# One tuned attention and feed-forward block: how rounded q and k travel to DRAM, and which engine turns four layer norms

## The chip, the cores and the metric

The program runs on one core of one Trainium2 chip. The metric is the device time of one execution in microseconds (us). Three executions of the kernel before took 732.46, 733.01 and 734.0 us; their median is 733.01 us. A profile was taken of one further execution.

## The reference

One transformer block on 2048 tokens of 448 features, in float32:

```python
def _A_ref(x, wqkv, wo):
    B, S, D = x.shape
    H = 16; Dh = D // H; W = 256
    qkv = ((x @ wqkv).reshape(B, S, 3, H, Dh)).transpose(2, 0, 3, 1, 4)
    q, k, v = qkv[0], qkv[1], qkv[2]
    scores = jnp.einsum("bhqd,bhkd->bhqk", q, k) * (Dh ** -0.5)
    mask = (i - j >= 0) & (i - j < W)
    p = _softmax(jnp.where(mask, scores, -1e9))
    o = jnp.einsum("bhqk,bhkd->bhqd", p, v)
    return o.transpose(0, 2, 1, 3).reshape(B, S, D) @ wo

h  = x + _A_ref(_layernorm(x), A_wqkv, A_wo)
n  = _layernorm(h)
h2 = h + (gelu(n @ w_gate) * (n @ w_up)) @ w_down      # 448 -> 1792 -> 448
```

There are 16 heads of 28 features, and a query sees the 256 tokens that end with itself.

## The kernel before

**Precision.** Matmuls run on a rounded float32 type (`F32R`). To keep float32 accuracy each operand is split in a high part (a copy rounded by ScalarE, `to_hi`, L342) and a low part (the rest, `to_lo`, L345, on VectorE or GpSimd), and a product is the sum of high x high, high x low and low x high. For q and k the three partial products sit side by side in the contraction: q is stored as (high, low, high) and k as (high, high, low), so that one matmul of 84 rows (3 x 28) makes a score tile.

**Stages.** The tokens go in 4 chunks (c) of 512, the heads in 4 groups (g) of 4. A block B = 4c + g is one chunk and one group, B = 0 to 15. Per chunk:

- `layer_norms` and `normalise` (L360, L387) make the normalised tokens of a 128-token tile t in `xn`, and its transpose in `xT`, high and low part. There are two ways. A tile that is not in `TURNED` is transposed by TensorE: four matmuls against `ident` (L398) into a PSUM bank, from which ScalarE takes the high part (L423) and VectorE the low part (L408, L409). A tile in `TURNED` goes through `turn` (L429): VectorE transposes 32x32 blocks into the other `xn` buffer (L435), four DMAs write them to DRAM in the right places (L439), two DMAs read the transposed tile back into `xT` (L441, L443), and then ScalarE makes the high part in three instructions (L447 to L449) and VectorE the low part in two (L452, L453). The layer norms ahead of the feed-forward (`kind == "ln2"`) always go through `turn`.
- `project_tile(c, m)` (L598) makes one of the 7 q and k tiles of a chunk: 11 matmuls (L609) into a PSUM bank, the high part by ScalarE (L613), the low part by VectorE (L614), both into a staging buffer that `pk_at` (L584) hands out in turn, and then DMAs to DRAM (`put`, L617). Even m are q of a group, odd m are k; each tile also holds 16 rows of k of the last group. There are two staging buffers in `proj`; tiles 2 and 3 (`PKX`) use a place in `pp`.
- `loads(B)` (L629) reads q and k of the block back from DRAM into `rq` and `rk` (L639), 84 rows by 4 heads.
- `scores` (L649) computes scores for the row maxima alone (matmul L657, VectorE L661), `maxima` (L671) turns these and puts them beside q (matmul L688), `probs` (L721) computes the scores again, transposed and with the maximum taken off (matmul L729), and ScalarE takes exp into `pp` (L733); `select` (L738) masks on GpSimd; `attend` (L753) multiplies by v (L763); `drain` and `output` divide and project (L788 to L810).

**Feed-forward.** 14 weight records of 128 columns; `product` (L954) does gate and up (L969 for the first four, L945 after them), gelu, and the down product, with VectorE adding to `hres` (L1047). Records 0 and 1 are fetched into `raw` (L864), record 2 through a DRAM copy (L857, key `FETCH`); their split is in `weight_splits` (L866). The first four products may run while attention is still going; they read records 0 and 1.

**What sets the order.** Every piece of work is an `op` with an engine, an estimated cost, a priority key and its dependences. `Lists.run` (L129) plays all of them through a model of the core while the program is built: again and again it takes, of all engines, the operation that can start first, the smallest key among those that can start at nearly the same moment, and emits it. So the instruction order of every engine, SyncE's DMA issues included, is fixed at build time by estimates; on the chip, semaphores only make an instruction wait. A block is 16 units of key. Constants shift keys:

```python
WIN = 14
LEAD = 90
LN1 = (0, -20, 70, 134)
LN2 = (166, 231)
FETCH = 200
PKX = (2, 3)
TURNED = (8, 9, 10, 11, 12, 13, 14, 15)
```

`WIN` is how far ahead of a block's need the matmuls of its projection begin (L608); `LN1[c]` is the key of the layer norms of chunk c; `LN2` and `LEAD` those of the layer norms ahead of the feed-forward.

**PSUM.** Eight banks of 128 x 512. `allowed` (L1132) says which kind of work may take which: until projections are done, scores have banks 0 and 1, probabilities 2 and 3, the attention sums 4 and 5, and layer norms that TensorE turns, v, projections and the output share 6 and 7.

Of the kernel before, what the change touches and what calls it, by code (L numbers as in the profile page):

```python
# [9 lines left out]
F32R = mybir.dt.float32r  # L10
# [18 lines left out]
WT = 7  # L29
# [6 lines left out]
LAG_P = 15  # L36
LAG_V = 10
EDGE = 8
WIN = 14
FFN = 1000  # L40
LEAD = 90
MARGIN = 0.8
START = 0.8
EARLY = 2
# [1 line left out]
HOLDO = 1  # L46
AHEAD = 7
BEHIND = 5
LN1 = (0, -20, 70, 134)
LN2 = (166, 231)  # L50
VKEY = (-30, -22, 14, 24)
VHALF = 0
FETCH = 200
POOLED = (3,)
PKX = (2, 3)
PAIRED = 4
TURNED = (8, 9, 10, 11, 12, 13, 14, 15)
SPANS = {"pp", "proj", "raw", "xT", "h", "rqf", "rkf", "vm", "rec0", "rec1", "rec2", "gh"}
SLOW = 9.0
WARM = 26.0  # L60
# [7 lines left out]
def mm(n):  # L68
    return max(n / 2400 + 0.0155, 0.115)
# [14 lines left out]
class Lists:  # L84
# [6 lines left out]
    def op(self, eng, cost, lat, key, fn, r=(), w=(), bank=None, port=False, size=0, tag=None, after=(), part=None):  # L91
        o = Op()
        o.eng, o.cost, o.lat, o.key, o.fn, o.port, o.size, o.tag = eng, cost, lat, key, fn, port, size, tag
        o.deps, o.users, o.ready, o.start = set(after), [], 0.0, None
        o.banks = () if bank is None else tuple(bank) if type(bank) is list else (bank,)
        for b in o.banks:
            b.left += 1
        held = o.banks if part is None else [(b, *part) for b in o.banks]
        if eng == "pe":
            w = (*w, *held)  # L100
        else:
            r = (*r, *held)
        for toks, wr in ((r, False), (w, True)):
            for tok in toks:
                spans = type(tok) is tuple and (tok[0] in SPANS or type(tok[0]) is Bank)
                name, lo, hi = tok if spans else (tok, 0, 1)
                old = self.seen.setdefault(name, [])
                keep = []
                for a in old:
                    if a[0] < hi and lo < a[1] and a[2] is not o:  # L110
                        if wr or a[3]:
                            o.deps.add(a[2])
                        if wr and lo <= a[0] and a[1] <= hi:
                            continue
                    keep.append(a)
                keep.append((lo, hi, o, wr))
                self.seen[name] = keep
        for d in o.deps:
            d.users.append(o)
        self.ops.append(o)  # L120
        if tag is not None:
            self.open[tag] = self.open.get(tag, 0) + 1
            self.all.setdefault(tag, []).append(o)
        return o
# [101 lines left out]
def block_kernel(ctx: ExitStack, tc, x, wqk_in, wv_in, wo_in, ffn_in, out):  # L226
    nc = tc.nc
# [9 lines left out]
    def f(ap):  # L237
        return ap.bitcast(F32)
# [7 lines left out]
    raw_m = pool.tile([128, 1472], F32, name="raw")  # L246
# [26 lines left out]
    pp_m = lp.tile([128, 4 * PPB * 128], F32, name="pp")  # L273
# [16 lines left out]
    pp = pp_m.rearrange("p (j t) -> p j t", j=4)  # L290
# [9 lines left out]
    pk = proj_m[:, 3584:5632].rearrange("p (a t) -> p a t", a=4)  # L300
# [5 lines left out]
    def span(name, lo, n):  # L306
        return (name, lo, lo + n)
# [9 lines left out]
    def PK(a):  # L317
        return span("proj", 3584 + 512 * a, 512)

    def WQK(m, h):  # L320
        return ("wqk", m, h)
# [20 lines left out]
    def to_hi(dst, src):  # L342
        nc.scalar.activation(dst, src, AF.Copy)  # L343

    def to_lo(dst, src, hi, eng=None):  # L345
        (eng or nc.vector).tensor_sub(dst, src, f(hi))

    def dma(key, size, fn, r=(), w=(), cost=0.44, after=()):
        return op("sp", cost, 0, key, fn, r, w, size=size, after=after)
# [37 lines left out]
    def normalise(t, key, kind):  # L387
        moved = kind == "ln2" or t in TURNED
        i2, i4 = 0 if moved else t % 2, t % 4
        b = None if moved else Bank(kind)  # L390

        def norm():
            nc.scalar.activation(xn[i2], hres[:, t, :], AF.Identity, scale=bnve[:, 1, i4:i4 + 1],
                                 bias=bnve[:, 2, i4:i4 + 1])

        def tr():
            for n, o in enumerate((0, 128, 256, D - 128)):
                nc.tensor.transpose(bank[b.k][:, n * 128:(n + 1) * 128], xn[i2][:, o:o + 128], ident)  # L398

        tc = col(t)  # L400
        c = slice(tc * 128, (tc + 1) * 128)

        def view():
            return bank[b.k].rearrange("p (b t) -> p b t", b=4)

        def lo():
            p = view()
            to_lo(xT[:, 4:7, c], p[:, 0:3], xT[:, 0:3, c])  # L408
            to_lo(xT[0:64, 3, c], p[64:128, 3], xT[64:128, 3, c])  # L409

        def norm_pool():
            nc.gpsimd.tensor_scalar(xn[i2], hres[:, t, :], bnve[:, 1, i4:i4 + 1], bnve[:, 2, i4:i4 + 1], op0=OP.mult,
                                    op1=OP.add)

        if kind == "ln1" and t in POOLED:
            op("pool", 1.0, 1.1, key, norm_pool, [HR(t), ("bnve", i4)], [("xn", i2)], port=True)
        else:
            op("act", 0.7, 0.76, key, norm, [HR(t), ("bnve", i4)], [("xn", i2)])
        if moved:
            turn(t, key, kind)  # L420
            return
        op("pe", 0.44, 0.61, key, tr, [("xn", i2), "ident"], (), b)
        op("act", 0.49, 0.605, key, lambda: to_hi(xT[:, 0:4, c], view()), (), [XT(tc)], b)  # L423
        op("dve", 0.89, 0.87, key, lo, [XT(tc)], [XT(tc)], b)
# [154 lines left out]
           [WQKRAW(m % 2), WQK(m, 0)], [WQK(m, 1)], port=True)  # L579


    pks = [0]

    def pk_at():  # L584
        n = pks[0]
        pks[0] += 1
        if n in PKX:
            o = 1792 + 1024 * PKX.index(n)
            return [pp_m[:, o + 512 * i:o + 512 * i + 512].bitcast(F32R) for i in range(2)], \
                pp_m[:, o:o + 1024].rearrange("p (a t) -> p a t", a=2), [span("pp", o // 128 + 4 * i, 4) for i in range(2)]  # L590
        n = sum(k not in PKX for k in range(n)) % 2
        return [pk[:, 2 * n + i] for i in range(2)], f(pk[:, 2 * n:2 * n + 2]), [PK(2 * n + i) for i in range(2)]

    def project(c):
        for m in range(WT):
# [2 lines left out]
    def project_tile(c, m):  # L598
        g, s = divmod(m, 2)
        cc = 12 * (c % 2)  # L600
        hl, both, tok = pk_at()
        B = 4 * c + g
        b = Bank("proj")
        per = 1 if m == 6 else 2
        base = 16 * B - EDGE
        for a in range(NP):
            h, wb, xb = TERMS[a]
            key = -33 + 6 * m + a / 4 if B < 2 else base - WIN * (1 - (s * NP + a) / (per * NP))  # L608
            op("pe", mm(512) + 0.002, 0.403, key, lambda a=a, h=h, wb=wb, xb=xb: nc.tensor.matmul(  # L609
                bank[b.k], wqk[m][:, h, wb, :], xT[:, xb, cc * 128:cc * 128 + 512], start=(a == 0),  # L610
                stop=(a == NP - 1)), [span("xT", cc, 4), WQK(m, h)], (), b, tag="proj")
        key = -30 + 6 * m if B < 2 else base
        op("act", 0.49, 0.605, key, lambda: to_hi(hl[0], bank[b.k]), (), [tok[0]], b)  # L613
        op("dve", 0.603, 0.698, key, lambda: to_lo(hl[1], bank[b.k], hl[0]), [tok[0]], [tok[1]], b)  # L614


        def put(rows, d, name, s, size):  # L617
            dma(key, 458 * size, lambda: nc.sync.dma_start(d[:, s:s + 2], both[rows]), tok, [(name, 0)])
            dma(key, 229 * size, lambda: nc.sync.dma_start(d[:, 2 - 2 * s], both[rows, 0]), tok[0:1], [(name, 1)])
        put(slice(0, GF), qk_d[g][c][s], ("d", g, s, c), s, 1)  # L620
        put(slice(GF, 128), qk_d[NG - 1][c][1][16 * m:16 * m + 16], ("d", NG - 1, 1, c, m), 1, 0.15)

# [231 lines left out]
    def weight_load(i, key, after=()):  # L854
        if i == 2:

            dma(FETCH, 1472, lambda: nc.sync.dma_start(ffn_d, ffn_in[i]), (), ["ffnd"], after=[got[NB - 4]])  # L857
            get, rat, opened = RECS[i]
# [211 lines left out]
    def ln1(c):  # L1070
        for i, n in ((0, 1), (1, 1), (2, 2)) if c == 0 else ((0, 2), (2, 2)):
            layer_norms(range(4 * c + i, 4 * c + i + n), lambda t: (LN1[c] - (0 if c else 40)) + (3 if c else 2) * (t % 4), "ln1")

    def ln2(c):
        for t in range(4 * c, 4 * c + 4, 2):
            layer_norms(range(t, t + 2), lambda t: LN2[c] + t % 4 if c < 2 else FFN + 30 * t - LEAD, "ln2")

# [144 lines left out]
```

## Time and profile before

| | before |
|---|---|
| median of three runs, us | 733.01 |
| the profiled execution, us | 733.24 |
| its span, first to last instruction, us | 731.5 |
| TensorE clock granted | 1.00 |
| VectorE busy, us | 404.7 |
| ScalarE busy, us | 368.0 |
| GpSimd busy, us | 155.7 |
| DMA packets | 102801 |
| moved by DMA, MB | 83.80 |
| chain that ended last: PE | 91% |

The profile is of one execution. An engine is busy while one of its instructions is in flight; matmuls overlap, so that a new one starts before the one ahead has ended, and a TensorE that is busy all the time can still start its matmuls later than it could. Where that matters, the distance from one matmul's start to the next one's is read from the timeline. "PEld" is the load of a matmul's stationary operand. In the timeline each row has a start in us from the first instruction, a length in us, the engine and line, the operation, out<-in, a count, and in brackets the idle time of the engine just before it and what ended that. SPq rows are DMA issues on SyncE's queue. 1.74 us of the 733.24 lie outside the span.

### The profile page before, as it was taken

What the parts mean: (1) busy time and instruction counts of PE and PEld (TensorE: products, weight loads), DVE (VectorE), ACT (ScalarE), POOL (GpSimd) and SP (SyncE); (2) the same over time, 40 slices, a digit from 0 to 9 for tenths busy, and PEclk for the clock granted to TensorE, in tenths of its full rate; (3) what the DMA queues carried; (4) which work ended last, traced back from release to release, by engine and by line L of the source; (5) the groups of instructions that cost most, each with busy time, mean ns of one, the idle gap of its engine ahead of it and who ended that gap; (6) DMA issues with size and microseconds to landing.
All of it is one profiled execution on the core that took longest, in us unless ns stands there. A gap on an engine that the chain in (4) does not pass through costs nothing.

```text
span 731.5 us, 15121 instructions
## 1 busy us (share of the span) xinstructions
PE 719.3 (98%) x5732; PEld 594.6 (81%) x5732; DVE 404.7 (55%) x1069; ACT 368.0 (50%) x934; POOL 155.7 (21%) x250
## 2 busy tenths in 40 slices
PE   8999999999999999999999999999999999999997
PEld 7886777777778787778888888888888888888886
DVE  7967778978798768858454223144223243233224
ACT  7647667787787678985443222243222233222221
POOL 5505443444344346541000000000000000000000
PEclk9999999999999999999999999999999999999999
DMA  8887787696677868341832000012100000001012
GB/s 307 268 269 234 207 251 184 179 260 200 176 184 196 224 190 239 86 111 26 199 120 84 1 1 3 1 42 84 43 1 1 2 1 1 2 1 51 7 46 101
DMA packets 102801, 83.80 MB, mean 115 GB/s; under 512 B 49272, under 2 KB 92472, under 8 KB 102712
## 3 DMA queue, kind: packets, MB, share of 16 engines
q1 hardware_dynamic: 102584, 82.72, 39.3%
q8 instruction: 45, 0.74, 0.4%
q14 instruction: 28, 0.23, 0.1%
q10 hardware_dynamic: 144, 0.11, 0.0%
HBM read 51.09 MB, written 31.95 MB: 114 GB/s over the span
## 4 chain that ended last, share of the span: by engine, by line
PE 91%; DMA 3%; ACT 3%; DVE 1%; issue 1%; SPq 0%; POOL 0%; DVEq 0%; ACTq 0%; POOLq 0%
PE bank L945 52%; PE bank L609 9%; PE bank L729 6%; PE bank L657 6%; PE bank L807 5%; PE bank L763 5%; PE bank L564 5%; PE bank L969 2%; DMA k<-proj 1%; ACT pp L733 1%; DMA xT<-xn 1%; DMA hres<-in_x_dram 1%; ACT xT L343 1%; ACT rq L343 0%; DMA xn<-xn 0%
## 5 line engine op out<-in xcount | busy, mean ns | idle before, releaser
L661 DVE CUSTOM_DVE_ANT_0 mt<-bank,mt 128x384 bf16<-128x384 f32 (+2 forms) x256 | 127.4, 525 | 33.0 <-PE bank L657 30.7
L733 ACT ACTIVATE pp<-bank 128x384 f32<-128x384 f32 (+2 forms) x352 | 123.0, 387 | 42.8 <-PE bank L729 37.4
L1011 DVE TENSOR_TENSOR mt<-bank,mt 128x512 f32<-128x512 f32 x54 | 37.1, 687 | 142.9 <-ACT mt L1009 142.9
L729 PE MATMUL bank<-rq,rk 104*128 104x384 f32 (+2 forms) x352 | 99.7, 306 | 3.1 <-ACT pp L733 1.7
L744 POOL TENSOR_SCALAR_AFFINE_SELECT pp<-pp 128x512 f32<-128x512 f32 x120 | 75.3, 641 | 110.3 <-ACT pp L733 108.7
L609 PE MATMUL bank<-xT 128*128 128x512 f32 x308 | 96.2, 401 | 0.0
L1009 ACT ACTIVATE mt<-bank 128x512 f32<-128x512 f32 x54 | 32.2, 596 | 118.3 <-PE bank L945 118.3
L729 PEld LDWEIGHTS bank<-rq,rk 104*128 104x128 f32 x352 | 65.3, 189 | 21.2 <-ACT pp L733 9.0
L945 PE MATMUL bank<-xT,rec 64*128 64x512 f32 x656 | 82.0, 388 | 0.0
L945 PE MATMUL bank<-xT,rk 64*128 64x512 f32 x656 | 82.0, 388 | 0.0
L657 PE MATMUL bank<-rk,rq 84*128 84x384 f32 (+2 forms) x256 | 80.3, 342 | 1.0 <-DMA rk<-k 0.8
L945 PEld LDWEIGHTS bank<-xT,rec 64*128 64x128 f32 x656 | 63.0, 184 | 12.2
L945 PEld LDWEIGHTS bank<-xT,rk 64*128 64x128 f32 x656 | 63.0, 184 | 12.2
L1047 DVE TENSOR_TENSOR hres<-bank,hres 128x448 f32<-128x448 f32 (+1 forms) x65 | 35.7, 610 | 66.5 <-PE bank L945 64.7
L945 PE MATMUL bank<-xT,proj 64*128 64x512 f32 x533 | 66.7, 388 | 0.3 <-ACT word L951 0.3
L951 ACT ACTIVATE word<-bank 1x1 f32<-1x1 f32 x162 | 25.6, 158 | 82.2 <-PE bank L945 81.6
L609 PEld LDWEIGHTS bank<-xT 128*128 128x128 f32 x308 | 55.7, 189 | 6.6 <-ACT xT L343 0.2
L945 PEld LDWEIGHTS bank<-xT,proj 64*128 64x128 f32 x533 | 51.1, 184 | 10.5 <-ACT word L951 0.6
L657 PEld LDWEIGHTS bank<-rk,rq 84*128 84x128 f32 x256 | 46.7, 189 | 11.7 <-issue 2.9
L564 PE MATMUL bank<-proj,xT 128*128 128x448 f32 (+1 forms) x220 | 51.1, 336 | 0.0
L343 ACT ACTIVATE rq<-bank 8x512 fp32r<-8x512 f32 x64 | 37.5, 586 | 17.6 <-PE bank L688 16.6
L763 PE MATMUL bank<-pp,v 128*29 128x384 f32 (+2 forms) x704 | 45.4, 388 | 0.0
(138 smaller groups left out, 1086.8 us busy)
## 6 DMA issues: line engine op xcount, KB each, us to landing
rk<-k SPq DMA_DIRECT2D x44, 336.0 KB
rq<-q SPq DMA_DIRECT2D x32, 336.0 KB
q<-proj SPq DMA_DIRECT2D x15, 448.0 KB
v<-in_ffn_dram SPq DMA_DIRECT2D x7, 736.0 KB
k<-proj SPq DMA_DIRECT2D x11, 448.0 KB
xn<-xn SPq DMA_DIRECT2D x88, 56.0 KB
xT<-xn SPq DMA_DIRECT2D x24, 192.0 KB
raw<-in_ffn_dram SPq DMA_DIRECT2D x6, 736.0 KB
```

The costliest lines, as they stand in the source:

```text
L343: nc.scalar.activation(dst, src, AF.Copy)
L564: op("pe", mm(224 * n), 0.29 if n == 1 else 0.38, key + a / 16, lambda a=a, h=h, wb=wb, xb=xb: nc.tensor.matmul(bank[b.k][:, 0:224 * n], x ...
L609: op("pe", mm(512) + 0.002, 0.403, key, lambda a=a, h=h, wb=wb, xb=xb: nc.tensor.matmul(bank[b.k], wqk[m][:, h, wb, :], xT[:, xb, cc * 128 ...
L657: nc.tensor.matmul(bank[b.k][:, o:384], rq[u][0:3 * DH, j, i * 128:i * 128 + 128], rk[u][0:3 * DH, j, m0 * 128:(i + 3) * 128], start=True, ...
L661: nc.vector.tensor_tensor_reduce(junk[s % 2][:, o:384], bank[b.k][:, o:384], mask[:, o:384], 1.0, -BIG, OP.add, OP.max, mx[i // 2][:, i % ...
L729: nc.tensor.matmul(bank[b.k][:, 0:n], rk[u][0:104, j, m * 128:m * 128 + 128], rq[u][0:104, j, lo * 128:(hi + 1) * 128], start=True, stop=True)
L733: nc.scalar.activation(pp[:, j, o * 128:o * 128 + n], bank[b.k][:, 0:n], AF.Exp, scale=SCALE)
L744: nc.gpsimd.affine_select(a, a, pattern=[[0, 4], [-cm, 128]], compare_op=op_, fill=0.0, base=0, channel_multiplier=cm)
L763: nc.tensor.matmul(bank[b.k][32 * j:32 * j + DH + 1, lo * 128:(hi + 1) * 128], v[:, at_v(4 * c - 2 + m), 4 * g + j, :], pp[:, j, at[m] * 1 ...
L807: op("pe", mm(D), 0.38, wk, lambda a=a, h=h, oh=oh, wh=wh, i=i, k=k: nc.tensor.matmul(bank[k.k][:, 0:D], ohl[:, h, oh, i * 128:(i + 1) * 1 ...
L945: nc.tensor.matmul(bank[bk.k][:, 0:n], w, m, start=bool(start), stop=bool(stop), tile_position=(64 * x, 0), skip_group_check=True)
L1011: op("dve", 0.605, 0.702, key + 2 * NP, lambda: nc.vector.tensor_tensor(blocks(g2), src(1), blocks(g2), op=OP.mult), [*G2, *held[1]], G2, ...
```

## The change

Three things change.

1. **The way of q and k to DRAM.** `put` still issues two DMAs for each range of rows, of twice and once the size. Before, the larger took the staged high and low part together (and waited for both), the smaller the high part again. Now the larger writes the high part to both of its places from one source read twice, and needs the high part alone; the smaller writes the low part.
2. **A third staging buffer.** From the last tile of the first chunk on (`n >= WT - 1`), `pk_at` goes round three buffers; the third is the first 1024 columns of `raw`, which holds weights being split before that and feed-forward records after it.
3. **Tiles 8 to 11 leave `TURNED`**, so the third chunk's layer norms are transposed by TensorE; and the key constants are set anew: `WIN`, `LEAD`, `LN1[2]`, `LN2[1]`, `FETCH`.

```diff
-WIN = 14
+WIN = 8
 FFN = 1000
-LEAD = 90
+LEAD = 100
...
-LN1 = (0, -20, 70, 134)
-LN2 = (166, 231)
+LN1 = (0, -20, 55, 134)
+LN2 = (166, 220)
...
-FETCH = 200
+FETCH = 240
+PKS = 3
...
-TURNED = (8, 9, 10, 11, 12, 13, 14, 15)
+TURNED = (12, 13, 14, 15)
...
-    pks = [0]
+    pks, ring = [0], [0]
 
     def pk_at():
         n = pks[0]
         pks[0] += 1
         if n in PKX:
-            o = 1792 + 1024 * PKX.index(n)
-            return [pp_m[:, o + 512 * i:o + 512 * i + 512].bitcast(F32R) for i in range(2)], \
-                pp_m[:, o:o + 1024].rearrange("p (a t) -> p a t", a=2), [span("pp", o // 128 + 4 * i, 4) for i in range(2)]
-        n = sum(k not in PKX for k in range(n)) % 2
-        return [pk[:, 2 * n + i] for i in range(2)], f(pk[:, 2 * n:2 * n + 2]), [PK(2 * n + i) for i in range(2)]
+            m, o, name = pp_m, 1792 + 1024 * PKX.index(n), "pp"
+        else:
+            k = ring[0]
+            ring[0] = (k + 1) % (2 if n < WT - 1 else PKS)
+            if k < 2:
+                return [pk[:, 2 * k + i] for i in range(2)], f(pk[:, 2 * k:2 * k + 2]), [PK(2 * k + i) for i in range(2)]
+            m, o, name = raw_m, 0, "raw"
+        unit = 128 if name == "pp" else 1
+        return [m[:, o + 512 * i:o + 512 * i + 512].bitcast(F32R) for i in range(2)], \
+            m[:, o:o + 1024].rearrange("p (a t) -> p a t", a=2), \
+            [span(name, (o + 512 * i) // unit, 512 // unit) for i in range(2)]
...
         def put(rows, d, name, s, size):
-            dma(key, 458 * size, lambda: nc.sync.dma_start(d[:, s:s + 2], both[rows]), tok, [(name, 0)])
-            dma(key, 229 * size, lambda: nc.sync.dma_start(d[:, 2 - 2 * s], both[rows, 0]), tok[0:1], [(name, 1)])
+            n = rows.stop - rows.start
+            dma(key, 458 * size, lambda: nc.sync.dma_start(
+                d[:, 0:3 - s:2 - s], both[rows, 0:1].to_broadcast([n, 2, 512])), tok[0:1], [(name, 0)])
+            dma(key, 229 * size, lambda: nc.sync.dma_start(d[:, 1 + s], both[rows, 1]), tok[1:2], [(name, 1)])
```

## The prediction

> **What bounds the kernel now.** I read the page's first part, then sums over stretches of time, then TensorE's waits, then the timeline around those waits.
>
> ```profile
> PE 719.3 (98%) x5732; PEld 594.6 (81%) x5732; DVE 404.7 (55%) x1069; ACT 368.0 (50%) x934; POOL 155.7 (21%) x250
> ...
> 50.00:120.00 70.00, 66.97 (x421) 51.33 (x419) 52.96 (x192) 50.78 (x123) 30.01 (x41) 1.00 0.78 224
> 120.00:200.00 80.00, 79.19 (x554) 61.37 (x554) 65.17 (x211) 61.92 (x158) 35.26 (x52) 1.00 0.72 197
> 200.00:285.00 85.00, 84.15 (x598) 67.89 (x595) 67.82 (x226) 64.97 (x167) 41.14 (x62) 1.00 0.74 200
> 285.00:330.00 45.00, 44.25 (x322) 32.66 (x321) 32.09 (x94) 39.88 (x107) 24.59 (x35) 1.00 0.51 128
> 330.00:731.50 401.50, 397.54 (x3571) 339.97 (x3569) 145.19 (x242) 119.32 (x328) 3.06 (x8) 1.00 0.12 37
> ```
>
> The columns of the stretches are length, busy time of TensorE, its weight loads, VectorE, ScalarE and GpSimd with counts, granted clock, DMA share, GB/s. TensorE is the bound everywhere at full clock. The change touches 50 to 330 us. There TensorE idles 3.03 + 0.81 + 0.85 + 0.75 = 5.4 us, more than half of it in the first stretch, where the third chunk's layer norms are being prepared. That is about the most a better order can give back, plus what hides in matmuls that start late behind a modelled end. The last stretch is the feed-forward, whose 4.0 us idle I leave as they are, since the change moves only `LEAD` there.
>
> Two of these idles sit on layer norm tiles that the change moves. The first, in the timeline at 79 us:
>
> ```profile
> 78.95 1.71 PE L564 MATMUL bank<-proj,xT 128*128 128x448 f32 x7
> ...
> 79.21 0.55 DVE L346 TENSOR_TENSOR xT<-xT 128x384 fp32r<-128x384 f32 x1
> ...
> 79.80 1.12 DVE L346 TENSOR_TENSOR xT<-xT,lasthi 64x128 fp32r<-64x128 f32 x1
> ...
> 81.84 0.28 PE L688 MATMUL bank<-one,mhl 128*72 128x128 f32 x1 [1.18 <-DVE mhl L681]
> 81.95 1.02 PE L564 MATMUL bank<-proj,xT 128*128 128x448 f32 x4
> 82.81 0.34 PE L657 MATMUL bank<-rk,rq 84*128 84x128 f32 x2
> ```
>
> VectorE spends 79.21 to 80.92 on the low part of tile 8, the turn of the maxima comes late, and TensorE stands. Four L564 matmuls take 82.81 - 81.95 = 0.86, so 0.215 each; seven take 1.5, but 81.84 - 78.95 is 2.89: **1.4 us** lost. The second, at 119 us:
>
> ```profile
> 118.42 0.44 PE L729 MATMUL bank<-rq,rk 104*128 104x384 f32 x1
> ...
> 118.70 0.52 ACT L343 ACTIVATE xT<-xT 128x384 fp32r<-128x384 f32 x1
> 118.91 0.45 PE L657 MATMUL bank<-rk,rq 84*128 84x384 f32 x1
> ...
> 119.57 0.31 ACT L343 ACTIVATE xT<-xT 64x128 fp32r<-64x128 f32 x1
> ...
> 120.30 0.81 PE L729 MATMUL bank<-rq,rk 104*128 104x384 f32 x2 [0.94 <-ACT pp L733]
> ```
>
> Three ScalarE instructions for tile 10's high part, 118.70 to 119.88, hold back an exp and with it the next L729. From 118.42 to 120.30 are 1.88 us for two matmuls of 384 columns; even at the 0.23 that a matmul of 512 takes (below), 1.88 - 0.46 = **1.4 us** are lost. A third wait is on a load of k:
>
> ```profile
> PE bank L657 <- DMA rk<-k: 0.8, 1, 0.8
> ...
> 237.53 3.65 SPq L439 DMA_DIRECT2D xn<-xn  x4
> ```
>
> SyncE spends 3.65 us issuing the four writes of one turned tile, among the loads of the coming block.
>
> **The change, part by part.** *Tiles 8 to 11 on TensorE.* TensorE gains 16 transposes:
>
> ```profile
> 20.74 0.60 PE L398 MATMUL bank<-ident,xn 128*128 128x128 f32 x4
> 21.09 1.87 PE L609 MATMUL bank<-xT 128*128 128x512 f32 x7
> 22.80 0.60 PE L398 MATMUL bank<-ident,xn 128*128 128x128 f32 x4
> 23.15 2.10 PE L609 MATMUL bank<-xT 128*128 128x512 f32 x8
> 25.09 0.60 PE L398 MATMUL bank<-ident,xn 128*128 128x128 f32 x4
> L398 PE MATMUL bank<-ident,xn 128*128 128x128 f32 x32 | 5.2, 292 | 0.7 <-ACT xn L393 0.7
> ```
>
> Start to start, 22.80 - 20.74 = 2.06 holds four transposes and seven L609, 25.09 - 22.80 = 2.29 four and eight. So an L609 is 0.23 and four transposes 0.45; four tiles are **+1.8 us**. All of it is on the path, since TensorE is the bound. The upper bound is the whole record, 0.292 each: 16 of them are 4.7.
>
> [...]
>
> The other engines get rid of work:
>
> ```profile
> L343 ACT ACTIVATE xT<-xT 128x384 fp32r<-128x384 f32 (+1 forms) x48 | 19.9, 414 | 0.5
> L343 ACT ACTIVATE lasthi<-xT 64x128 fp32r<-64x128 f32 x24 | 7.4, 308 | 0.6
> L343 ACT ACTIVATE xT<-bank 128x512 fp32r<-128x512 f32 x8 | 4.6, 587 | 0.3 <-PE bank L398 0.3
> L435 DVE STREAM_TRANSPOSE xn<-xn 128x448 f32<-128x448 f32 x22 | 13.9, 633 | 1.5 <-DMA xn<-xn 1.3 <-ACT xn L393 0.2
> L346 DVE TENSOR_TENSOR xT<-bank,xT 128x384 fp32r<-128x384 f32 (+1 forms) x16 | 6.8, 424 | 0.3
> ```
>
> ScalarE: (19.9 + 7.4) / 24 = 1.14 a tile becomes 0.59, four tiles -2.2 us. VectorE: for tile 8 the transpose, 0.63, and the low part, 0.55 + 1.12 by the rows at 79 us, become 2 x 0.42 = 0.85. SyncE loses six issues a tile and their traffic. None of that is on the path by itself; it counts through the waits. Both waits above are behind the very instructions that go. I take them as gone: **-2.8**. What is late next is the rest of TensorE's waits for ScalarE: in 50 to 120 us its weight loads wait 1.5 + 1.3 us for exps and for maxima being put beside q. ScalarE's lighter load and the smoother mix from a smaller `WIN` may take some; I take **-0.4**, between nothing and 2.8.
>
> ```profile
> PEld bank L729 <- ACT pp L733: 1.5, 5, 0.5
> PEld bank L729 <- ACT rq L343: 1.3, 3, 0.6
> ```
>
> *Third buffer and order of the copies.* The same bytes move. SyncE before already issued the copy that needs only the high part first:
>
> ```profile
> 66.13 0.79 SPq L619 DMA_DIRECT2D k<-proj  x2
> ...
> 67.02 0.84 SPq L618 DMA_DIRECT2D k<-proj  x2
> ```
>
> So only one more plane travels 0.9 us sooner, and what is left to wait for VectorE is half as large. No row among the waits of ScalarE or VectorE names a landing of these copies: the two buffers cost nothing that is visible as a wait; the plan had placed the evacuations after the landings. So this part can work only through a load that comes sooner. The one load that TensorE waits for costs 0.8; I take half, **-0.4**, since its load is behind writes of another layer norm that stay. The bounds are 0 and -0.8.
>
> *The keys.* `WIN` moves only the start of a projection's matmuls; the last keeps almost its key, base - 8/22 against base - 14/22, so loads are due when they were. `LN1[2]` lets four layer norms start sooner, two of whose last steps are the rows at 79 and 119 us. `LN2[1]` and `FETCH` move work between 200 and 330 us where TensorE idles 1.6; `LEAD` acts in the feed-forward. I put zero for these, with a bound of 1.0 either way from the 0.85 and 0.75 idle there.
>
> **Sum.** 1.8 - 2.8 - 0.4 - 0.4 = -1.8, and with what lies outside the span unchanged 733.24 becomes 731.4 for a profiled execution. That execution is 0.23 above the median of the runs, 733.01, so the median becomes **731.2 us**. Its own range goes down to 729.8 (the load's other 0.4, the keys' 1.0) and up to 731.5; what lies above is counted with the waits that move.
>
> **Rivals.** *The waits move.* The order of every engine is drawn up anew, so an exp or a maximum may be late elsewhere. If one of the two big waits returns, 731.2 + 1.4 = 732.6. For it: PE's rows list several such waits, all from ScalarE or VectorE, whose busy shares around 100 us are three quarters. Against it: the estimate of ScalarE's part of a turned tile, 0.7 in the code, is far below the 1.14 measured, while that of the new way, 0.49, is near 0.59; four badly planned pieces leave.
>
> *Transposes at full price.* Scattered one at a time among other matmuls, each could cost its 0.292: 731.2 + 4.7 - 1.8 = 734.1. [...]
>
> *All order, no cost.* If the idle of 50 to 285 us goes as a whole, 3.03 + 0.81 + 0.85 = 4.7, with what hides behind modelled ends (2.8 lost at the two waits against 1.18 + 0.94 marked idle) some 5.4: 733.0 + 1.8 - 5.4 = 729.4, and 728.0 if half of the weight loads' 2.8 goes too.
>
> *Slower: a bank held.* A tile turned by TensorE holds bank 6 or 7 from its first transpose until VectorE has read it, and the next chunk's projections, v and the output need the same two banks.
>
> ```profile
> 23.30 0.86 DVE L346 TENSOR_TENSOR xT<-bank,xT 128x384 fp32r<-128x384 f32 x2
> ```
>
> The tile whose transposes start at 20.74 is done at 24.16, a hold of 3.4 us. Four are 13.7 out of 140 bank-microseconds of the first stretch. If a late evacuation lets TensorE run out of matmuls with a free bank, the price is one wait of the size seen there, 1.18, per tile. Then three tiles give 1.8 - 2.8 + 3.5 = +2.5, 735.5; four 736.7. It decides from the second tile on (+1.4); with one, the sum is as before. Against it: scores and probabilities have their own banks and fill in.
>
> *Slower: late records.* The third buffer sits where feed-forward record 0 was fetched long ahead.
>
> ```profile
> 92.64 0.35 SPq L864 DMA_DIRECT2D raw<-in_ffn_dram  x1
> ...
> 261.66 0.60 ACT L343 ACTIVATE proj<-bank 128x512 fp32r<-128x512 f32 x1 [0.17 <-PE bank L609]
> ...
> 276.63 0.36 SPq L864 DMA_DIRECT2D raw<-in_ffn_dram  x1
> ...
> 281.98 0.63 ACT L343 ACTIVATE proj<-raw 128x512 fp32r<-128x512 f32 x1
> ...
> 285.26 0.39 PE L969 MATMUL bank<-xT,proj 128*128 128x512 f32 x1
> ```
>
> The sixth tile of the last chunk takes the third buffer until about 266, so record 0 can be fetched only then. Record 1's fetch to split is 281.98 - 276.63 = 5.4, so record 0's split would begin at 271.4; the first matmul that reads it is at 285.26. That hides unless the fetch slips by some ten microseconds, the split itself taking four or so; then TensorE lacks filler around 285 and loses perhaps the 2 to 3 us by which it is late: 735.
>
> *The change does nothing it says.* Copies and buffers may show no effect at all; then 0.4 of the sum goes, 731.6, on the line between faster and the same.
>
> **How the numbers follow.** A measurement of this kernel tells about 0.2% from no change, so faster is below 731.5 and slower above 734.5. Forecast 0.38, all order 0.10, half of the 0.08 for copies that do nothing: faster 0.52. The other half, waits that move 0.18, full price 0.06: same 0.28. Bank 0.12, late records 0.08: slower 0.20. The range leaves out about half of all order below and half of the slower cases above, some 0.15: 728.0 to 735.5.
>
> **What would show it.** L398 at 48 matmuls, the added sixteen at 0.11 apart; L439 at 80 issues instead of 96; no idle of over a microsecond in front of L688 or L729 between 50 and 125 us; TensorE's idle in 50 to 120 down from 3.0 to about 1; the wait L657 <- rk<-k gone or halved; record 0 fetched after 265 with the first L969 still near 285. New long waits behind ScalarE, a rise of L609's distances after transposes, or L969 starting after 288 would make the prediction wrong.

## The result, and the profile after

The changed kernel takes **729.64 us** (median of six runs, 729.59 to 729.77); the kernel before, run beside it, 733.46 us (six runs, 732.46 to 735.19). The ratio is 0.9947, interval 0.9934 to 0.996: 0.5% faster, some 3.8 us. The forecast was 731.2 us with a gain of 1.8, so the direction was right and the gain twice as large as its sum.

The profiled execution took 729.68 us with a span of 727.9; that of before had a span of 731.5. The 3.6 us to be explained lie inside the span. The page's busy times, its DMA total and the first line of the chain that ended last:

```profile
PE 720.1 (99%) x5748; PEld 596.8 (82%) x5748; DVE 398.7 (55%) x1065; ACT 364.0 (50%) x926; POOL 155.0 (21%) x250
...
DMA packets 96784, 81.82 MB, mean 112 GB/s; under 512 B 41720, under 2 KB 82872, under 8 KB 96696
...
PE 94%; ACT 3%; DVE 1%; issue 1%; DMA 0%; POOL 0%; DVEq 0%; ACTq 0%
```

TensorE has 16 more matmuls and 0.8 us more busy time (719.3 before), and yet the span is shorter: what went is idle time. The sums over the stretches used in the prediction (length, busy time of each engine, granted clock, DMA share, GB/s):

```profile
50.00:120.00 70.00, 69.62 (x442) 53.21 (x441) 52.97 (x197) 51.54 (x123) 29.00 (x39) 1.00 0.75 215
120.00:200.00 80.00, 79.54 (x569) 63.90 (x569) 64.74 (x222) 62.89 (x161) 35.97 (x55) 1.00 0.70 189
200.00:285.00 85.00, 84.92 (x614) 68.03 (x613) 66.29 (x220) 63.38 (x165) 42.19 (x63) 1.00 0.70 199
285.00:330.00 45.00, 44.20 (x300) 32.02 (x297) 32.51 (x87) 37.66 (x101) 23.03 (x32) 1.00 0.44 111
```

Idle in 50 to 330 us is 0.38 + 0.46 + 0.08 + 0.80 = 1.7 us; before it was 5.4, so 3.7 less. Over the whole span the idle time fell by 4.4 us, from 12.2 to 7.8, and the busy time rose by 0.8: together the span's -3.6. In 50 to 120 alone the idle time fell from 3.03 to 0.38. TensorE's waits (total us, times, longest):

```profile
PE bank L1179 <- POOL ident L491: 2.1, 1, 2.1
PE bank L739 <- ACT pp L743: 0.6, 2, 0.3
PE bank L739 <- ACT rq L344: 0.3, 1, 0.3
PE bank L399 <- ACT xn L394: 0.2, 1, 0.2
PE bank L979 <- ACT v L1004: 0.2, 1, 0.2
PE bank L667 <- DVE mx L671: 0.2, 1, 0.2
```

Lines have moved: L688, L729, L657, L609, L343, L398 and L969 of before are L698, L739, L667, L617, L344, L399 and L979 here. The first wait is the start of the kernel, the same as before. The waits of 1.2 us for the turned maxima (L688) and of 0.8 for a load of k (L657) are gone, and no other single wait is above 0.3.

### The profile page after: what moved, and what is told of

It is laid out like the page before. It is cut to its first block, busy times and chain, and to the rows that moved or that the text cites. A ratio compares the mean times of both kernels' runs of the same rounds, so it can differ in the third digit from the quotient of the medians.

```text
span 727.9 us, 15062 instructions
## 1 busy us (share of the span) xinstructions
PE 720.1 (99%) x5748; PEld 596.8 (82%) x5748; DVE 398.7 (55%) x1065; ACT 364.0 (50%) x926; POOL 155.0 (21%) x250
## 4 chain that ended last, share of the span: by engine, by line
PE 94%; ACT 3%; DVE 1%; issue 1%; DMA 0%; POOL 0%; DVEq 0%; ACTq 0%
PE bank L955 53%; PE bank L617 9%; PE bank L739 7%; PE bank L667 6%; PE bank L773 6%; PE bank L817 5%; PE bank L565 5%; PE bank L979 3%; PE bank L399 1%; ACT rq L344 1%; ACT pp L743 1%; ACT xT L344 0%; ACT rk L344 0%; PE bank L698 0%; DMA hres<-in_x_dram 0%
## 5 line engine op out<-in xcount | busy, mean ns | idle before, releaser
L739 PE MATMUL bank<-rq,rk 104*128 104x384 f32 (+2 forms) x352 | 97.9, 305 | 1.4 <-ACT pp L743 0.6
L617 PE MATMUL bank<-xT 128*128 128x512 f32 x308 | 95.1, 402 | 0.0
L739 PEld LDWEIGHTS bank<-rq,rk 104*128 104x128 f32 x352 | 65.0, 189 | 20.0 <-ACT pp L743 4.9
L667 PE MATMUL bank<-rk,rq 84*128 84x384 f32 (+2 forms) x256 | 80.5, 340 | 0.2 <-DVE mx L671 0.2
L955 PEld LDWEIGHTS bank<-xT,rk 64*128 64x128 f32 x656 | 63.0, 184 | 12.2
L955 PEld LDWEIGHTS bank<-xT,rec 64*128 64x128 f32 x656 | 62.9, 184 | 12.2
L617 PEld LDWEIGHTS bank<-xT 128*128 128x128 f32 x308 | 55.5, 189 | 7.1 <-issue 0.2
L667 PEld LDWEIGHTS bank<-rk,rq 84*128 84x128 f32 x256 | 46.7, 189 | 9.6 <-issue 2.7
L344 ACT ACTIVATE rq<-bank 8x512 fp32r<-8x512 f32 x64 | 37.5, 586 | 15.8 <-PE bank L698 14.8
```

What stands on the lines that cost most here:

```text
L667: nc.tensor.matmul(bank[b.k][:, o:384], rq[u][0:3 * DH, j, i * 128:i * 128 + 128], rk[u][0:3 * DH, j, m0 * 128:(i + 3) * 128], start=True, ...
L739: nc.tensor.matmul(bank[b.k][:, 0:n], rk[u][0:104, j, m * 128:m * 128 + 128], rq[u][0:104, j, lo * 128:(hi + 1) * 128], start=True, stop=True)
L955: nc.tensor.matmul(bank[bk.k][:, 0:n], w, m, start=bool(start), stop=bool(stop), tile_position=(64 * x, 0), skip_group_check=True)
```

## The experiments

Each kernel's ratio is against the kernel before, run beside it on the same chip.

### The three parts, alone and in pairs

The change is cut in three: the tiles 8 to 11 turned by TensorE, the five keys, and the copies with their third buffer.

```diff
# tiles alone, in the kernel before (turned_only)
-TURNED = (8, 9, 10, 11, 12, 13, 14, 15)
+TURNED = (12, 13, 14, 15)
# keys alone, in the kernel before (keys_only)
-WIN = 14
+WIN = 8
-LEAD = 90
+LEAD = 100
-LN1 = (0, -20, 70, 134)
-LN2 = (166, 231)
+LN1 = (0, -20, 55, 134)
+LN2 = (166, 220)
-FETCH = 200
+FETCH = 240
# copies alone (copies_only): the change's pk_at and put, with
+PKS = 3
# all but the tiles, in the kernel after (all_but_turned)
-TURNED = (12, 13, 14, 15)
+TURNED = (8, 9, 10, 11, 12, 13, 14, 15)
```

The pairs put the same pieces together: `turned_copies` is the kernel after with the old keys, `turned_keys` the kernel before with both the tiles and the keys.

> The kernel before with TURNED = (12, 13, 14, 15) alone. If the waits behind tiles 8 and 10 carry the gain: +1.8 for sixteen transposes and -2.8 for two waits, so 1 us faster than before, and no wait of over a microsecond on L688 or L729 between 50 and 125 us. If the keys carry it: nothing but the price of the transposes, 1 to 2 us slower. If the third buffer and the order of the copies carry it: the same, 1 to 2 us slower.

> The kernel before with the five key constants of the change (WIN, LEAD, LN1, LN2, FETCH) alone. If the keys carry the gain: 3 us or more faster than before. By the prediction: within 1 us of before, either way.

> The kernel before with the third buffer and the new order of the copies, old keys, tiles 8 to 11 turned by DMA. By the prediction: 0 to 0.8 us faster than before. If the copies carry the gain: 3 us or more faster.

> The changed kernel with tiles 8 to 11 turned by DMA as before; the copies, the third buffer and the keys are the new ones. If the waits behind tiles 8 and 10 carry the gain: about 1 us slower than the changed kernel, 730.6 where that is 729.6. If the keys or the copies carry it: faster than the changed kernel by the 1.8 of the transposes, 727.8.

> The changed kernel with the old five keys: tiles 8 to 11 turned by TensorE, third buffer and new copies. If copies and keys do nothing by themselves once the tiles are turned by TensorE: 730.7 as turned_only, within 1. If the copies carry what is left of the gain: 729.6 as the changed kernel. If the copies harm as they did alone: 4 to 6 us above 730.7.

> The kernel before with tiles 8 to 11 turned by TensorE and the five new keys, old copies and two buffers. If the keys carry what is left of the gain: 729.6 as the changed kernel. If nothing: 730.7 as turned_only, within 1. If the keys harm as they did alone: 3 to 4 us above 730.7, with the granted clock at 0.5 somewhere in its trace.

| parts | median, us | ratio to before | interval |
|---|---|---|---|
| tiles | 730.71 | 0.9966 | 0.9954 to 0.9977 |
| keys | 737.02 | 1.0046 | 1.0028 to 1.0065 |
| copies | 738.9 | 1.007 | 1.0048 to 1.0092 |
| copies, keys | 742.34 | 1.0121 | 1.0099 to 1.0143 |
| tiles, copies | 733.96 | 1.0002 | 0.9983 to 1.0022 |
| tiles, keys | 733.89 | 0.9999 | 0.9986 to 1.0013 |
| all three | 729.64 | 0.9947 | 0.9934 to 0.996 |

The parts do not add up. Turning the tiles gains in every one of the four pairs (none to tiles, keys to tiles and keys, and so on: 0.3, 0.5, 0.7 and 1.7% of the time before). The copies and the keys lose wherever they stand without each other or without the tiles, and gain only on top of the other two. The prediction gave copies -0.4 and keys 0 with a bound of 1.0 us either way; alone they cost 0.7 and 0.46%, which is 5.1 and 3.4 us. Copies and keys without the tiles were expected about 1 us above the changed kernel; they are 12.7 above it (742.34 against 729.64), which no expectation foresaw. The next experiments look for what moves the time by such amounts when the work hardly changes.

### The instructions of four tiles taken out, the order kept

To test the two waits without a new order, this kernel leaves the plan untouched and issues none of the five instructions that make the high and low part of tiles 8 to 11.

```diff
-        op("act", 0.7, 0.82, key + 0.2, hi, (), [XT(tc), "lasthi"])
+        op("act", 0.7, 0.82, key + 0.2, (lambda: None) if kind == "ln1" and 8 <= t < 12 else hi, (), [XT(tc), "lasthi"])
```

and the same for `lo` on VectorE. The kernel thus leaves out the high and the low part of four tiles and gives no right result for them; only its time is of use here.

> The kernel before, leaving out the five instructions that make the high and the low part of tiles 8 to 11 (three of ScalarE, two of VectorE a tile), with the plan, its costs and the order of everything else as they are; the features of those four tiles are then not computed. The prediction's theory: TensorE's two waits, 1.4 us each at 82 us (L688) and at 120 us (L729), are behind just these instructions. They go, with some of the shorter waits for ScalarE, and the time falls by 2.8 us or a little more, to 730.0 to 730.8 at full clock. Rival, the waits have another cause, or move to the next late instruction: less than 1.0 us is gained, 732.3 or more, and a wait of over a microsecond stands in front of L688 near 82 or of L729 near 120 us. A value between says how much of the 2.8 these instructions carry.

Measured: 730.09 us (729.49 to 732.22, 7 runs), ratio 0.9958, interval 0.9944 to 0.9973. TensorE's timeline, first around the place of the L688 wait, then around that of the L729 wait (start, length, engine and line, operation, operands, count):

```profile
80.58 1.68 PE L564 MATMUL bank<-proj,xT 128*128 128x448 f32 x7
82.10 0.22 PE L688 MATMUL bank<-one,mhl 128*72 128x128 f32 x1
...
118.45 0.44 PE L729 MATMUL bank<-rq,rk 104*128 104x384 f32 x1
118.95 0.44 PE L657 MATMUL bank<-rk,rq 84*128 84x384 f32 x1
119.27 0.83 PE L729 MATMUL bank<-rq,rk 104*128 104x384 f32 x2
```

From the seven L564 to L688 are 82.10 - 80.58 = 1.52 us, before 2.89: 1.37 us less. From the L729 at 118.45 to the two that follow are 0.82, before 1.88: 1.06 less. So these instructions carry **2.4 us** of waiting at just these two places, close to the 2.8 of the prediction, and no late instruction took their place there. (The ratio is worth 3.1 us; the profiled execution also has 3.41 us at half clock from 67.6 us on, of which more below.) The rows of its waits show what stayed, because the order stayed:

```profile
PE bank L729 <- ACT rq L343: 1.0, 3, 0.5
PE bank L657 <- DMA rk<-k: 1.0, 1, 1.0
```

The wait for the load of k and three ScalarE waits near 65 us are still there. In the changed kernel they are gone too, and they make the rest of the surplus.

### The transposes issued twice

```diff
-            for n, o in enumerate((0, 128, 256, D - 128)):
+            for n, o in (2 if t > 7 else 1) * list(enumerate((0, 128, 256, D - 128))):
```

> The changed kernel with each of the sixteen added transposes of tiles 8 to 11 issued twice, in the same order and at the same planned cost. The prediction's term of 1.8 us for sixteen, 0.11 each on the path: 729.6 + 1.8 = 731.4. Rival, full price of 0.292 each: 729.6 + 4.7 = 734.3. Rival, TensorE has slack where they stand and they cost nothing: 729.6 to 730.1.

Measured: 730.64 us (730.61 to 730.7, 5 runs), 1.0 us above the changed kernel. The group at 60 us in the changed kernel:

```profile
60.51 0.66 PE L399 MATMUL bank<-ident,xn 128*128 128x128 f32 x4
60.92 0.30 PE L698 MATMUL bank<-one,mhl 128*72 128x128 f32 x1
```

and with the transposes doubled:

```profile
61.13 1.09 PE L399 MATMUL bank<-ident,xn 128*128 128x128 f32 x8
61.98 0.30 PE L698 MATMUL bank<-one,mhl 128*72 128x128 f32 x1
```

0.41 us for four, 0.85 for eight: 0.11 for each more, as the prediction took it. Sixteen should then cost 1.8; at the end 1.0 was left. Compared matmul by matmul in the two traces, the doubled kernel is 0.8 us behind at 62 us, just after the last of the four groups, and 0.8 to 1.0 from there to the end: the rest was taken up between the groups, not by the waits further on. The full record, 0.29 apiece, is ruled out as the price here.

### True costs in the plan

The prediction noted that the plan put ScalarE's part of a turned tile at 0.7 us where 1.14 was measured. If that error made the waits, the kernel before with the measured costs would lose them.

```diff
-        op("act", 0.7, 0.82, key + 0.2, hi, (), [XT(tc), "lasthi"])
-        op("dve", 0.75, 0.82, key + 0.2, lo, [XT(tc), "lasthi"], [XT(tc)], port=True)
+        op("act", 1.14, 1.26, key + 0.2, hi, (), [XT(tc), "lasthi"])
+        op("dve", 0.87, 0.94, key + 0.2, lo, [XT(tc), "lasthi"], [XT(tc)], port=True)
```

> The kernel before with the plan's costs of a DMA-turned tile set to what the trace shows: the high part 1.14 instead of 0.7, the low part 0.87 instead of 0.75; the work is the same. If the two waits came from a plan that took these pieces for shorter than they are: 1 to 3 us faster than before, without one of TensorE's transposes. If they come from the work itself: within 0.5 of before.

Measured: 735.09 us, ratio 1.002, interval 1.0004 to 1.0035: some 1.2 us slower, which neither expectation foresaw. Three of the rows of its waits:

```profile
PE bank L657 <- DVE mx L661: 0.9, 2, 0.6
PE bank L729 <- ACT pp L733: 0.8, 3, 0.4
PE bank L688 <- DVE mhl L681: 0.5, 1, 0.5
```

With the work unchanged, the wait at L688 shrank from 1.18 to 0.49 us, and the one of 0.94 at L729 near 120 us to 0.20 (timeline); two waits at L657 for VectorE's maxima are new. So the plan's low costs had a part in the two waits, beside the work itself. But the right costs also drew a new order, and what it gained at these places it lost at others: by the sum further down its waits are 8.6 us, against 8.3 before. "Four badly planned pieces leave" is therefore neither refuted nor enough.

### Filled gaps: is it the clock?

The slowest combination, copies and keys without the tiles, shows stretches at half the granted clock. Its 3.41 us stretches from 98.85 us on (the last three columns are clock, DMA share, GB/s):

```profile
98.85:102.27 3.42, 3.42 (x30) 2.58 (x29) 3.08 (x10) 0.98 (x2) 0.61 (x1) 1.00 0.71 220
102.27:105.68 3.41, 2.63 (x12) 1.55 (x10) 3.35 (x13) 3.08 (x9) 1.05 (x2) 1.00 0.97 327
105.68:109.09 3.41, 2.96 (x8) 2.18 (x9) 2.45 (x11) 2.56 (x6) 2.17 (x3) 0.50 0.29 80
109.09:112.51 3.42, 3.40 (x16) 2.03 (x19) 2.54 (x9) 2.88 (x7) 2.13 (x4) 0.50 0.93 298
112.51:115.92 3.41, 3.41 (x18) 1.86 (x11) 0.98 (x4) 0.82 (x4) 0.00 (x0) 0.50 0.50 135
115.92:119.33 3.41, 3.41 (x33) 2.68 (x32) 2.59 (x10) 2.17 (x8) 1.17 (x2) 1.00 0.43 128
```

Ahead of the drop is one stretch with 12 matmuls in place of 30 and 0.78 us idle; three stretches at 0.50 follow. With another drop of 6.83 us near 300, 17.1 us ran at half clock, which is 8.5 us of full-clock time. The test lets the kernel's own filler (a transpose of `ident` into a free bank wherever the plan leaves TensorE idle, allowed up to 26 us) go on to 320 us. It adds 87 transposes, more than the some fifty expected; the order of the other engines stays.

```diff
-WARM = 26.0
+WARM = 320.0
```

> The kernel all_but_turned (742.3 us) with WARM = 320 instead of 26: where the plan leaves TensorE idle up to 320 us it now issues a transpose of ident whose result nobody reads, some fifty in all; the other engines keep their order. In that kernel's trace the granted clock is 0.5 for 10.24 and 6.83 us. If the half clock is what makes it slow, and is caused by TensorE's waits: the fifty transposes, 5 us of work at 0.11 each, remove it, and the kernel is 4 to 8 us faster than 742.3. If the waits themselves are what makes it slow: the same or up to 5 us slower.

Measured: 738.3 us against 742.34 (ratio to before 1.0066, interval 1.0044 to 1.0087), with 5819 matmuls instead of 5732. The stretch that had 12 matmuls:

```profile
102.27:105.68 3.41, 3.24 (x21) 2.75 (x20) 3.35 (x13) 3.10 (x8) 1.05 (x1) 1.00 1.01 335
```

The mean clock of the profiled execution is 1.000, without the filler 0.988. Over four executions each it is 0.998 to 1.000, without the filler 0.988 to 0.990. The gain of 4.0 us is at the lower edge of what was expected. The filler is work too: 87 transposes at 0.11 us are 9.6. So this order had a twofold price: its waits, and the half clock behind them, 17.1 us of it, which was gone when the gaps were filled.

### A new order with the same work

Last, how much does a new order alone do? `MARGIN` is the plan's allowance for the landing of a load. Moving it changes no work, only the places of some instructions.

```diff
-MARGIN = 0.8
+MARGIN = 0.81
```

> The kernel before with MARGIN, the planner's allowance for the landing of a load, at 0.81 instead of 0.8: no work is changed, only some places in the order. How much does a redrawn order alone move the time? If the gain of the change is the work that it takes off VectorE and ScalarE, this stays within 1.0 us of 733.0 and the spread is small against 3.6. If the gain is mostly a matter of which order happens to be drawn, it moves by 2 us or more, in either direction, and most where the granted clock falls.

> The changed kernel with MARGIN at 0.81 instead of 0.8, as above: no work is changed, the order is drawn anew from about 60 us on. If the gain belongs to the change, 729.6 to 731.0, still ahead of the kernel before. If it belongs to this one order, 732 to 737, with TensorE's waits back between 50 and 330 us or with some microseconds at half clock.

Measured: the kernel before goes from 733.89 to 736.12 us (ratio 1.0037, interval 1.0022 to 1.0052). The changed kernel goes to 733.97 (1.0006, 0.9994 to 1.0017): **the whole gain over the kernel before with its old margin is lost**; against the kernel before with the same new margin 2.2 us are left. TensorE's waits in the kernel before with the new margin, the largest ones:

```profile
PE bank L729 <- ACT pp L733: 2.5, 5, 1.0
...
PE bank L688 <- DVE mhl L681: 1.2, 1, 1.2
PE bank L729 <- ACT rq L343: 1.0, 3, 0.5
...
PE bank L969 <- DVE rq L346: 0.7, 1, 0.7
```

The wait at L688 is still there, more exps are late, and a wait of 0.7 at L969 is new. In the changed kernel the L688 wait stays away with the new margin too, but an exp is late at 292 us (timeline), and a stretch at half clock stands right behind it (stretches):

```profile
290.32 0.43 PE L667 MATMUL bank<-rk,rq 84*128 84x384 f32 x1
292.23 0.60 PE L739 MATMUL bank<-rq,rk 104*128 104x256 f32 x2 [1.48 <-ACT pp L743]
```

```profile
291.15:294.57 3.42, 2.17 (x11) 1.78 (x12) 2.37 (x7) 3.36 (x10) 3.07 (x6) 1.00 0.54 111
294.57:297.98 3.41, 3.41 (x12) 2.84 (x10) 0.00 (x0) 2.44 (x9) 2.58 (x4) 0.50 0.86 207
```

### All kernels in one sum

For every profiled execution two things are added up. *Waits*: for each matmul that starts between 26 and 340 us, its distance from the start of the one ahead, less what the one ahead usually takes, put at 0.23 us for 512 columns and in proportion for fewer (median distances in the trace of the kernel before, 26 to 340 us: 0.233 us for 512 columns, 0.205 for 448, 0.177 for 384, 0.116 for 256, 0.060 for 128); only excesses above 0.25 us count, and none from half-clock stretches. *Clock*: half the length of the stretches at half clock between 26 and 340 us. The rest is the span less both.

| kernel | span | waits | clock | rest |
|---|---|---|---|---|
| before | 731.5 | 8.3 | 0 | 723.2 |
| before, new margin | 733.7 | 10.6 | 0 | 723.1 |
| parts of four tiles left out | 730.5 | 5.9 | 1.7 | 722.9 |
| tiles | 730.0 | 4.6 | 1.7 | 723.7 |
| keys | 736.1 | 10.6 | 3.4 | 722.1 |
| copies | 737.3 | 7.8 | 5.1 | 724.4 |
| copies, keys | 741.5 | 10.4 | 8.5 | 722.6 |
| copies, keys, 87 transposes as filler | 736.3 | 6.0 | 0 | 730.3 |
| before, measured costs in the plan | 732.4 | 8.6 | 0 | 723.8 |
| tiles, copies | 732.3 | 5.8 | 3.4 | 723.1 |
| tiles, keys | 732.2 | 7.9 | 1.7 | 722.6 |
| after | 727.9 | 3.4 | 0 | 724.5 |
| after, new margin | 732.3 | 5.7 | 1.7 | 724.9 |
| after, transposes doubled | 728.9 | 3.4 | 0 | 725.5 |

But for the kernel with filler, whose transposes are counted in it, the rest stays within 722.1 to 725.5, while the span moves by 13.6 us. What the parts of the change do to the time is nearly all waits and clock. For the change itself: waits 8.3 to 3.4, so -4.9, and rest +1.3; together the span's -3.6. The +1.3 is no price of the transposes: the five kernels that have the same sixteen of them differ by 2.3 in the rest, from 722.6 to 724.9.

## Why the prediction was right, and where its sizes were off

The measured 729.64 lies inside the stated range of 728.0 to 735.5, but just below 729.8, where the forecast's own terms end. That the sum came out on the right side is in part luck: its terms for keys and copies, near zero, fit neither part alone, and the same change with the margin at 0.81 takes 733.97, which the prediction would have called the same.

- **The bound, and where the time would come from: right.** Of the 4.4 us by which TensorE's idle time fell, 3.7 lie in 50 to 330 us, most of them in 50 to 120. SyncE's writes of turned tiles (L439) fell from 96 to 80, as foreseen.
- **The two waits, -2.8: right, and shown.** With the instructions left out and the order kept, 2.4 us go at these two places. Neither wait is in the changed kernel. Right costs in the plan also shorten them, so the instructions are not their only cause.
- **Sixteen transposes, +1.8: right in mechanism, probably too large at the end.** 0.11 us each where they stand; a second set of sixteen costs 1.0 at the end. What the first set costs was not measured by itself. The group in the changed kernel answers to the prediction's row:

```profile
L399 PE MATMUL bank<-ident,xn 128*128 128x128 f32 x48 | 7.9, 294 | 0.2 <-ACT xn L394 0.2
```

- **Other waits for ScalarE, -0.4: the term that was mis-sized.** Three waits of the kernel before near 65 us went as well, with 0.67, 0.44 and 0.61 by the measure above, 1.7 us together:

```profile
64.92 0.45 PE L729 MATMUL bank<-rq,rk 104*128 104x384 f32 x1 [0.45 <-ACT rq L343]
65.53 0.44 PE L729 MATMUL bank<-rq,rk 104*128 104x384 f32 x1 [0.16 <-ACT rq L343]
65.81 0.34 PE L657 MATMUL bank<-rk,rq 84*128 84x128 f32 x2
66.54 0.44 PE L729 MATMUL bank<-rq,rk 104*128 104x384 f32 x1 [0.39 <-ACT pp L733]
```

The prediction saw them only as a part of the 2.8 us that weight loads wait, and took a seventh of that. They are not caused by the four tiles' instructions, since they stay where only those are left out; they went with the new order. What in the new order removed them was not tested.
- **The load wait, -0.4: right that it goes, whole (1.0 us by the same measure), wrong about why.** It is also absent with the tiles alone, where the copies are the old ones: that kernel's waits are

```profile
PE bank L1169 <- POOL ident L490: 2.1, 1, 2.1
PE bank L729 <- ACT pp L733: 1.9, 3, 1.3
PE bank L398 <- ACT xn L393: 0.9, 2, 0.6
PE bank L945 <- ACT word L951: 0.3, 1, 0.3
PE bank L969 <- ACT v L994: 0.2, 1, 0.2
```

with no load among them. So the copies are not needed for it. The fewer writes of the tiles are not needed either: in the kernel before with the measured costs in the plan, where tiles, copies and keys are all the old ones, no wait for a load is in the rows. A new order is enough.

- **Keys 0 +- 1.0 and copies 0 to -0.8: wrong as sizes of a part.** Alone they cost 3.4 and 5.1 us. The step that failed is the idea that a key or a buffer costs what its own work costs: it also draws a new order for all engines, and 0.01 in an allowance that changes no work moves the time by 2.2 and 4.3 us. How much of the 3.4 and 5.1 belongs to the keys and the copies as such, and how much to the draw, stays open; these runs cannot tell them apart.
- **The rivals.** "All order, no cost" foresaw 729.4 and is nearest in size, by the disappearance of most of the idle between 50 and 285 us (4.7 us became 0.9), though transposes are not free: a second sixteen cost 1.0. "The waits move" is what the other draws show: the changed kernel with the new margin has a 1.5 us wait at 292 us. A bank held does not show: no wait of TensorE in the list above names L347. Late records do not show either: record 0 is fetched and split here,

```profile
268.10 0.36 SPq L874 DMA_DIRECT2D raw<-in_ffn_dram  x1
...
278.10 1.62 ACT L344 ACTIVATE proj<-raw 128x512 fp32r<-128x512 f32 x3
```

and the first matmuls on it follow at 281.7 us, even sooner than the 285.26 of before:

```profile
L979 PE MATMUL bank<-xT,proj x27: 389/399/505, 281.7 to 300.0; 128*128 128x512 f32 x27
```

What a reader should take for the change's worth: with the old margin 3.8 us (733.46 to 729.64), with the new one 2.2 (736.12 to 733.97). Turning the tiles helped in all four pairs; how much the change brings in all depends on the order that is drawn.

## What to carry to other kernels

Where a plan draws the order of all engines from estimates, measure how far a meaningless change of a constant moves the time before any difference of that size is credited to an edit; here it was 0.4 to 0.6%, about as much as the whole gain. To test a suspected wait, take its cause out with the plan and the order held fixed: that gave 2.4 us for two waits, where every reordered variant mixed several effects. Moving a short burst of work to the engine that is the bound can pay, if it takes longer pieces off the engines that feed it at a moment when they are late: here the waits behind those pieces were worth 2.4 us, and sixteen more transposes cost 1.0.

## What the runs showed of the hardware that was not expected

**Half-clock stretches stood behind short waits.** The granted clock fell from 1.00 to 0.50 for multiples of 3.41 us (3.41, 6.83, 10.24). The stretch ahead of the longest, 102.27 to 105.68 us with copies and keys, still had 2.63 of 3.41 us busy; the timeline marks idles of 0.32, 0.25 and 0.21 us in it. In the kernel with the tiles alone a wait of 1.5 us with one of 0.4 behind it (marked idle: 1.31 and 0.16) stands ahead of a drop (same columns as above):

```profile
289.00:292.42 3.42, 2.14 (x10) 1.73 (x11) 2.07 (x6) 3.33 (x11) 3.09 (x7) 1.00 0.86 220
292.42:295.83 3.41, 3.41 (x12) 2.82 (x11) 1.34 (x3) 2.70 (x11) 2.06 (x3) 0.50 0.93 227
```

Busy time alone does not tell where a drop follows: the kernel before has a stretch nearly as thin, without a drop in that execution:

```profile
78.40:81.81 3.41, 2.26 (x23) 1.49 (x15) 3.35 (x9) 0.91 (x3) 1.38 (x2) 1.00 0.86 218
```

The trace of the kernel before gives the full clock from 7.17 to 730.80 us, which is 212 times 3.413; that of the changed kernel from 8.05 to 728.26, 211 times 3.413. With copies and keys the first drop lasts from 105.68 to 115.92 us, three times 3.413. Counted in steps of 3.413 us from 7.17 us on, the thin stretch of the kernel before runs from 78.85 to 82.27 and has 2.23 us busy, again without a drop; the stretches right ahead of the drops shown here had 2.14 (tiles), 2.17 (after, new margin) and 2.63 us (copies, keys). Whether a drop depends on how a wait falls on these steps was not tested.

The clock also orders the spread between 58 executions of the kernel before: those at a mean clock of at least 0.999 take 732.2 to 733.5 us, those at 0.995 or less 734.6 to 736.5. The changed kernel never fell below 0.999 in its six runs, and they lie within 0.2 us.

**The clock rose, and stayed up, on transposes.** With 87 transposes of `ident` in the gaps, the mean granted clock was 1.000 where it had been 0.988. Plainer is the start of the kernel before, where TensorE has nothing but transposes until 9.15 us:

```profile
2.13 4.10 PE L1169 MATMUL bank<-ident 128*128 128x128 f32 x18 [2.13 <-POOL ident L490]
...
8.25 1.15 PE L1169 MATMUL bank<-ident 128*128 128x128 f32 x9
```

The first eighteen start some 0.21 us apart, the nine 0.11; the trace puts the full clock from 7.17 us on. The trace lists these transposes as MATMUL; at L399 of the changed kernel a record is 294 ns long on average, and at the full clock it is 0.11 us from one start to the next.
